# Zero rows under the last key block, later reciprocals and a fourth step masked on VectorE in a top-k attention and expert kernel

## The chip, the cores and the metric

The kernel runs on one core of a Trainium2 chip. What is timed is the device time of one execution, in microseconds (us). TensorE is called PE here, VectorE DVE, ScalarE ACT, GpSimd POOL and SyncE SP, as the profile does. PEld is the weight load of a matmul, SPq the queue of transfers that SP issues.

## What is computed

Attention over 2 batches and 8 heads, 576 tokens, 64 numbers a head, in which each token keeps its 32 best scores; then a sum over four experts with given shares; then a gated layer. All is float32.

```
scores = scale * np.matmul(q, k.transpose(0, 1, 3, 2))
kth = np.partition(scores, -32, axis=-1)[..., -32:-31]
scores = np.where(scores >= kth, scores, -1e9)
attn = np.exp(scores - scores.max(-1, keepdims=True))
attn = attn / (attn.sum(-1, keepdims=True) + 1e-09)
x = (attn @ v) as 1152 x 512
for e in range(4): y += p[:, e:e+1] * (relu(x @ w1[e]) @ w2[e])
out = ((y @ w_a) * (y @ w_b)) @ w_out
```

## The kernel before, in words

The 1152 tokens are nine tiles of 128: four of each batch, and a mixed one (MIX) with the last 64 tokens of both batches. The tiles stand in four groups of 1, 2, 3 and 3. Attention runs in 36 **steps**, numbered from 0: for each group, for each of the four pairs of heads, for each tile of the group. So steps 0 to 3 are group 0, 4 to 11 group 1, 12 to 23 group 2, 24 to 35 group 3.

One step does this for both heads of its pair. `scores` (L553) multiplies queries and keys on PE and ACT copies the result out of PSUM (L582). `masked` (L587) finds the 32 best of each of the 128 rows on DVE, by four MAX8 (L603, eight best at a time) and three MATCH_REPLACE8 (L609, which strikes them out) for each head. POOL makes the two row constants (L649); ACT and POOL push every score below the 32nd far down (L656, L659), ACT takes the exponent and its sum (L666), POOL adds 1e-9 (L675), DVE takes the reciprocal (L676), ACT scales (L679). The result is called e here. `weigh` (L686) turns e on PE (five matmuls against an identity for each head, L365), ACT copies it out (L706, L710), and PE multiplies it with the values (L726). The keys of a head are four blocks of 128 and a rest of 64: the rest's matmuls use 64 rows of the array, the other blocks 128. All these matmuls of `weigh` fill 64 of the 128 columns, two heads side by side. After the last tile of a pair the sum goes to `xf` (group 0) or, split into a high and a low part, to `xs` (the other groups, L744 on ACT, L746 on DVE).

Step 3 is marked URGENT. Its POOL work is done on DVE instead and its ACT work goes ahead of everything else, since its end lets PE begin on the expert layer of group 0.

The expert layer follows group by group: `plain` (L888) for group 0 in full float32, with weights in the regions `raw` and `ys`; `experts` (L817) for the others, with weights split into two parts by ACT (L767) and by POOL or DVE (L768), and results taken out by ACT (L837) and DVE (L841, L859). A group's first expert matmuls need all four pairs' `xs`. `replace` turns a group's result back, and `gated` is the last layer.

The order is not written out by hand. Every piece is recorded as an `Op` with an engine, a modelled duration (`hold`), a lag until others see it, a key and its waits; `Plan.order` (L91) plays the pieces through with these durations, picks on each engine the ready one of lowest key, and emits the instructions of each engine in the order in which they came up. Attention has keys near its step's number, copies out of PSUM negative ones, expert work 500 and more. On the chip each engine then runs its list strictly in that order and waits on semaphores. DVE's list thus mixes top-k work with the copies of the expert layer, and PE's mixes attention with expert matmuls. SP's list holds all transfers, in order too.

Of the kernel before, what the change touches and what calls it, by code (L numbers as in the profile page):

```python
# [8 lines left out]
F32 = mybir.dt.float32  # L9
# [57 lines left out]
class Op:  # L67
    __slots__ = ("engine", "hold", "lag", "key", "emit", "waits", "after", "tiles", "n", "start", "left", "at", "nbytes", "port")
# [7 lines left out]
class Plan:  # L76
# [3 lines left out]
    def add(self, engine, hold, emit, key, after=(), tiles=(), lag=100, nbytes=0, port=False):  # L80
# [4 lines left out]
        op.after, op.n, op.start, op.nbytes, op.port = [], len(self.ops), None, nbytes, port  # L85
# [5 lines left out]
    def order(self):  # L91
        for op in self.ops:
            op.left, op.at = len(op.waits), 0.0
            for w in op.waits:
                w.after.append(op)
# [17 lines left out]
        queue, now, done = [], 0.0, []  # L113
# [124 lines left out]
PAIRED, URGENT = (), 3  # L238


def body(tc, q, k, v, probs, w1, w2, wa, wb, wo, out):
# [50 lines left out]
    vrem = [const(f"vrem{b}", [REM, H, D]) for b in range(B)]  # L292
# [14 lines left out]
    raw = Region("raw", 3 * 1024, F32)  # L307
    wraws = raw.slots("wraw", 3, 1024)
    low = Region("low", 12800, F32)
# [34 lines left out]
    def load(dst, src, key, after=(), tiles=(), nbytes=1 << 18):  # L344

        return plan.add("SP", 0, lambda: nc.sync.dma_start(out=dst(), in_=src()), key, after, tiles, nbytes=nbytes)
# [37 lines left out]
    def consts():  # L384
        make_identity(nc, ident)
        nc.vector.tensor_copy(identr, ident)
        nc.gpsimd.memset(qm.bitcast(F32), 0.0)
        nc.gpsimd.memset(facs[:, :, 0], -scale)
        nc.gpsimd.memset(facs[:, :, 1], STEEP)

    ready = gpsimd(1900, consts, -1e6, (), ())

    loads = []
    for i, t in enumerate(TILES):
        for rows_, view in token_rows(t, probs):
            loads.append(load(lambda i=i, rows_=rows_: pr[rows_, i], lambda view=view: view, 2.0, nbytes=4096))
# [7 lines left out]
    shared = vector(900, shares, 3.5, loads, ())  # L404
# [13 lines left out]
    def keys(b, h2, key, eng):  # L418
# [7 lines left out]
        if first_:  # L426
            sp = [split(lambda j=j: sv()[:, j, :, 0], lambda j=j: sv()[:, j, :, 1], lambda j=j: rv()[:, j], 256, key, [ld], [rt, st_], eng) for j in range(2)]
# [18 lines left out]
        for j in range(2):  # L446
            at = atts.tile(key + 0.02)
# [7 lines left out]
            o = tensor(5 * TURN_R, turn, key + 0.02, sp[j] + krem_done[b][h + j] + [ready], [at, st_])  # L455
# [7 lines left out]
        if any(c for c, g in enumerate(GROUPS) if (b, h2) not in kept and c >= 0):  # L463
            kept[b, h2] = load(
                lambda: kscr[b, h2], lambda: kt.ap.rearrange("p (j n) -> p j n", j=2).bitcast(F32), key + 1, got, [kt], 576 << 10
# [11 lines left out]
    def start_pair(c, h2, n):  # L477
# [32 lines left out]
        for j in range(2):  # L510
            src = lambda j=j: rqv()[:, j].unsqueeze(2).to_broadcast([128, m, 2, D])
            sp[j] += split(lambda j=j: sqv()[:, j, 0:m, 0], lambda j=j: sqv()[:, j, 0:m, 1], src, m * 128, key + 0.03, lds, [rq, sq], eng)
            if m < T:
                if not qrem_done:
                    for b in range(B):
                        qrem_done.append(load(lambda b=b: qrem[b * REM:(b + 1) * REM], lambda b=b: last_rows(q, b), key - 2, (), (), 131072))
# [26 lines left out]
        for b in batches(tiles):  # L543
# [3 lines left out]
                lambda vt=vt: vt.ap.rearrange("p (h m d) -> p h m d", h=2, m=M4), lambda b=b: main_rows(v, b, h), n - 2.5, (), [vt]  # L547
            )]
            if b not in vrem_done:
                vrem_done[b] = load(lambda b=b: vrem[b], lambda b=b: last_rows(v, b), n - 2.4, (), (), 131072)  # L550
        return pair

    def scores(pair, j, i, n):  # L553
# [24 lines left out]
        o = tensor(4 * len(bs) * mm_r(HALF), emit, n - AHEAD, after, [at] + used)  # L578
# [503 lines left out]
```

## Time and profile before

| | us |
|---|---|
| median of 3 runs (867.55 to 869.35) | 867.97 |
| the profiled execution, its time | 866.53 |
| its span in the profile | 864.7 |
| PE busy in the span | 826.5 |
| DVE busy | 715.8 |
| ACT busy | 544.6 |
| POOL busy | 265.2 |

A busy share is a mean over stages with different limits. The profile cuts the span into 40 slices; in the first three PE is busy for 5, 5 and 7 tenths, and then for 9 tenths or more (90% and above) in nearly all others. The view by line names the program's line, the engine, the operation, the tiles written and read, the count, busy time, and the idle time ahead of it. The timeline lists instructions by their start, with like neighbours merged; the bracket gives the idle time of that engine before the row and what ended it.

### The profile page before, as it was taken

Reading aid. Unit: us, or ns where it says so; the run is one execution under the profiler, and the core shown is the slowest. Engines: PE = TensorE matmul, PEld = TensorE weight load, DVE = VectorE, ACT = ScalarE, POOL = GpSimd, SP = SyncE. Lnnn points to the kernel's source line nnn. Section 1 sums busy time; section 2 is a strip of 40 time slices with the busy share of each in tenths; the row PEclk is TensorE's granted clock in tenths of the full one; section 3 lists DMA queues with packets and bytes.
Section 4 is the critical chain, followed back from the end, with each engine's and each line's share of the span. In section 5 each row is a group of like instructions: output and inputs, shape, how many; then the busy total and the mean of one; then the engine's idle time right before and its main releaser. Section 6 shows DMA issues by size and latency. Waiting matters only on the chain. (4 is left out here: it accounts for less than half of the span.)

```text
span 864.7 us, 14129 instructions
## 1 busy us (share of the span) xinstructions
PE 826.5 (96%) x5168; PEld 728.0 (84%) x5168; DVE 715.8 (83%) x1381; ACT 544.6 (63%) x1042; POOL 265.2 (31%) x245
## 2 busy tenths in 40 slices
PE   5579999999999999999999999999999999999997
PEld 4466777788888888889888888889999989999996
DVE  6899999999999999999978999555434888999723
ACT  5888987899989998877765655333324535344310
POOL 2634442887897965853320000000000000000000
PEclk9999999999999999999999999999999999999999
DMA  7727977844564444342234556434101313323003
GB/s 197 244 90 257 297 239 235 268 149 145 168 185 150 152 148 153 98 123 97 75 122 156 179 177 195 122 122 128 44 1 49 98 49 98 91 81 98 25 1 109
DMA packets 83509, 117.06 MB, mean 135 GB/s; under 512 B 10608, under 2 KB 54640, under 8 KB 83440
## 3 DMA queue, kind: packets, MB, share of 16 engines
q1 hardware_dynamic: 83440, 116.17, 42.9%
q8 instruction: 40, 0.66, 0.3%
q14 instruction: 29, 0.24, 0.1%
HBM read 109.07 MB, written 7.08 MB: 134 GB/s over the span
## 5 line engine op out<-in xcount | busy, mean ns | idle before, releaser
L603 DVE MAX8 low<-low 128x8 f32<-128x576 f32 x288 | 203.7, 747 | 3.4 <-ACT low L582 3.3
L362 PE MATMUL ps<-xs,mid 128*128 128x384 f32 (+1 forms) x1152 | 205.1, 322 | 1.3 <-POOL mid L768 1.0
L362 PE MATMUL ps<-mid 128*128 128x512 f32 x768 | 198.6, 396 | 2.1 <-DVE mid L841 2.0
L362 PEld LDWEIGHTS ps<-xs,mid 128*128 128x128 f32 x1152 | 184.4, 189 | 11.5 <-issue 2.5
L362 PEld LDWEIGHTS ps<-mid 128*128 128x128 f32 x768 | 139.2, 188 | 28.5 <-DVE mid L841 6.0
L609 DVE MATCH_REPLACE8 low<-low 128x576 f32<-128x576 f32 x216 | 159.3, 743 | 0.0
L362 PE MATMUL ps<-xs,big 128*128 128x384 f32 x864 | 152.8, 335 | 0.0
L362 PEld LDWEIGHTS ps<-xs,big 128*128 128x128 f32 x864 | 149.9, 188 | 1.6 <-DVE low L1033 0.3
L767 ACT ACTIVATE mid<-raw 128x1024 fp32r<-128x1024 f32 x96 | 101.5, 1059 | 66.3 <-issue 39.9
L768 POOL TENSOR_TENSOR mid<-raw,mid 128x1024 fp32r<-128x1024 f32 x48 | 115.2, 2408 | 11.9 <-ACT mid L767 8.9
L659 POOL TENSOR_TENSOR low<-low 128x576 f32<-128x576 f32 x70 | 98.9, 1428 | 32.8 <-ACT low L656 31.0
L362 PE MATMUL ps<-big,mid 128*128 128x512 f32 x324 | 75.1, 390 | 0.0
L768 DVE TENSOR_TENSOR mid<-raw,mid 128x1024 fp32r<-128x1024 f32 x48 | 58.5, 1220 | 18.9 <-ACT mid L767 18.7
L362 PEld LDWEIGHTS ps<-big,mid 128*128 128x128 f32 x324 | 60.7, 188 | 12.3
L837 ACT ACTIVATE mid<-ps 128x384 fp32r<-128x384 f32 (+1 forms) x96 | 42.7, 450 | 33.0 <-PE ps L362 28.3
L859 DVE SCALAR_TENSOR_TENSOR ys<-ps,pr,ys 128x512 f32<-128x512 f32 x56 | 41.5, 747 | 24.3 <-PE ps L362 23.7
L841 DVE SCALAR_TENSOR_TENSOR mid<-ps,mid 128x384 fp32r<-128x384 f32 (+1 forms) x96 | 48.0, 506 | 15.1 <-ACT mid L837 14.6
L656 ACT ACTIVATE low<-low 128x576 f32<-128x576 f32 x72 | 53.4, 772 | 7.6 <-POOL low L649 7.4
L1012 ACT ACTIVATE low<-ps 128x384 f32<-128x384 f32 x36 | 17.6, 489 | 64.1 <-PE ps L362 64.0
L365 PE MATMUL ps<-ident,low 128*128 128x128 f32 (+1 forms) x360 | 50.6, 282 | 7.3 <-ACT low L679 7.1
L679 ACT ACTIVATE low<-low 128x576 f32<-128x576 f32 x72 | 52.9, 776 | 6.1 <-DVE low L676 6.1
L666 ACT ACTIVATE low<-low 128x576 f32<-128x576 f32 x72 | 55.7, 774 | 0.7 <-POOL low L659 0.7
(76 smaller groups left out, 1040.0 us busy)
## 6 DMA issues: line engine op xcount, KB each, us to landing
raw<-in_moe_w_dram SPq DMA_DIRECT2D x120, 512.0 KB, 3.7
big<-kscr SPq DMA_DIRECT2D x20, 576.0 KB, 4.8
low<-in_v_dram SPq DMA_DIRECT2D x24, 256.0 KB, 4.1
low<-in_moe_w_a_dram SPq DMA_DIRECT2D x12, 512.0 KB, 3.8
low<-in_moe_w_b_dram SPq DMA_DIRECT2D x12, 512.0 KB, 3.8
low<-in_moe_w_out_dram SPq DMA_DIRECT2D x12, 512.0 KB, 3.6
kscr<-big SPq DMA_DIRECT2D x8, 576.0 KB, 4.4
ys<-in_moe_w_dram SPq DMA_DIRECT2D x8, 512.0 KB, 4.6
```

Of the source, the lines that this page charges most:

```text
L362: nc.tensor.matmul(out, l, r, **kw)
L365: nc.tensor.transpose(out, a, i)
L603: 62 + 1.04 * width, lambda at=at, cs=cs: nc.vector.max(m8v()[:, x, cs], at()), key + 0.02 * r, [done],
L609: lambda at=at, cs=cs: nc.vector.match_replace(out=src[1](), in_to_replace=m8v()[:, x, cs], in_values=at(), imm_value=LOW),
L656: S, lambda x=x, s=s: nc.scalar.activation(e[x].ap, s.ap, AF.Relu, bias=endv()[:, x, 1:2], scale=-STEEP),
L659: sub = lambda eng, x=x, s=s: eng.tensor_tensor(e[x].ap, s.ap, e[x].ap, op=ALU.subtract)
L666: lambda x=x: nc.scalar.activation(e[x].ap, e[x].ap, AF.Exp, bias=endv()[:, x, 0:1], scale=scale, accum_out=sums.ap[:, x:x + 1]),
L679: S, lambda x=x: nc.scalar.activation(e[x].ap, e[x].ap, AF.Copy, scale=sums.ap[:, x:x + 1]),
L767: hi = scalar(1024, lambda: nc.scalar.activation(u.ap[:, 0:1024], r.ap, AF.Copy), 500 + s, [ld], [u, r], sbuf=True)
L768: sub = lambda eng: eng.tensor_tensor(u.ap[:, 1024:2048], r.ap, u.ap[:, 0:1024], op=ALU.subtract)
L837: n, lambda h=h, p=p: nc.scalar.activation(h.ap[:, 0:n], p.ap[:, 0:n], AF.Relu), -1000, [o], [h, p]
L841: lambda h=h, p=p: nc.vector.scalar_tensor_tensor(h.ap[:, n:2 * n], p.ap[:, 0:n], 0.0, h.ap[:, 0:n], op0=ALU.max, op1=ALU.subtract),
```

## The change

- **Zero rows.** The tiles of the rest of the values (`vrem`) get 128 rows, and rows 64 to 127 of it and of the last block of the turned e (`pt`) are set to zero once, on POOL, near the start (five memsets). The matmuls of `weigh` on the rest use 128 rows of the array like the others. `weigh` waits for the zeros.
- **Later reciprocals.** The planner is told that the sum of a step is seen 1200 ns later (2400 ns for steps 0 and 1), so DVE's reciprocal stands later in its list. Its key is lower for steps 0 to 2.
- **Step 3 masked on DVE.** ACT takes the exponent of all scores as soon as the first eight maxima are known. After the last MAX8 DVE does, for each head, one SCALAR_TENSOR_TENSOR (score at least the 32nd, times the exponent, with the row sum), adds 1e-9, takes the reciprocal and scales with a TENSOR_SCALAR. The turn of its e gets a key ahead of most other PE work, and the ACT and POOL work of steps 0 to 2 gets lower keys.
- **Loads by time.** A transfer can be held back to a planned time (`since`): shares at 30 us, values from 9 us on, the weights of group 0 from 20 us on, the stored keys at 13 us, the queries' rest at 60 us.
- **Two engines evict first.** In step 0 DVE takes over two of the four copies out of PSUM that ACT did, the keys of the second head and the queries of the first, and the operands are split head by head.
- **Fourth weight place.** `raw` holds 4 tiles, not 3; room comes from the second identity and from `low`. Every fifth weight tile of group 0 goes to `ys`, not every fourth.
- **Planned durations.** The turn of a key pair is planned at 640 ns (440 before), of e at 516 (476), scores with 30 more, `weigh` at 1245 (1150).
- **Early units.** `experts` takes a weight unit out of a table `ahead` if there is one. Nothing is ever put into that table.

The diff, cut to its core:

```diff
-        queue, now, done = [], 0.0, []
+        queue, now, done = [(op.since, -1, None) for op in self.ops if op.since], 0.0, []
...
-    ident = const("ident", [128, 128])
     identr = const("identr", [128, 128], F32R)
+    ident = identr.bitcast(F32)
...
-    vrem = [const(f"vrem{b}", [REM, H, D]) for b in range(B)]
+    vrem = [const(f"vrem{b}", [128, H, D]) for b in range(B)]
...
-    raw = Region("raw", 3 * 1024, F32)
-    wraws = raw.slots("wraw", 3, 1024)
+    raw = Region("raw", 4 * 1024, F32)
+    wraws = raw.slots("wraw", 4, 1024)
...
+    def zeros():
+        for b in range(B):
+            nc.gpsimd.memset(vrem[b][REM:128], 0.0)
+        for p in pts.aps:
+            nc.gpsimd.memset(p[REM:128, MAIN:MAIN + 128], 0.0)
+    zeroed = gpsimd(1500, zeros, 0.2, [ready], ())
...
+            if first_ and j == 1:
+                got.append(vector(
+                    dve(S),
+                    lambda j=j, at=at: nc.vector.tensor_copy(kt.ap[:, j * S:(j + 1) * S], at.ap.rearrange("p a n -> p (a n)")[:, 0:S]),
+                    -902 + j, [o], [at, kt],
+                ))
+                continue
...
+        ks = n + 0.1 if n > URGENT else n - 0.7
...
+        sm.lag += 2 * SLACK if n < URGENT - 1 else SLACK
+        rc = vector(70, lambda: nc.vector.reciprocal(sums.ap, sums.ap), -500 if n > URGENT else -3500, [sm], [sums])
...
+    def hurried(sd, n, m8v, m8, ends, endv, sums, firsts, last):
...
+            ex = scalar(
+                S, lambda x=x, s=s, e=e: nc.scalar.activation(e.ap, s.ap, AF.Exp, bias=endv()[:, x, 0:1], scale=scale),
+                n + 0.1, [en], [s, e, ends], sbuf=True, ptr=True,
+            )
+            sv = lambda x=x: sums.ap[:, x:x + 1]
+
+            def mask(x=x, s=s, e=e, sv=sv):
+                nc.vector.scalar_tensor_tensor(
+                    e.ap, s.ap, m8v()[:, x, TOPK - 1:TOPK], e.ap, op0=ALU.is_ge, op1=ALU.mult, accum_out=sv()
+                )
+                nc.vector.tensor_scalar(sv(), sv(), 1e-9, None, op0=ALU.add)
+                nc.vector.reciprocal(sv(), sv())
+                nc.vector.tensor_scalar(e.ap, e.ap, sv(), None, op0=ALU.mult)
+            out_.append((e, vector(1450, mask, -3000, [ex, last[x]], [s, e, m8, sums], port=True)))
...
-            at, p = atts.tile(n + 0.5), pts.tile(n)
+            kt = n + (-0.06 if n == URGENT else 0.5)
+            at, p = atts.tile(kt), pts.tile(n)
...
-                        l, rows = (vt[:, j, m], 128) if m < M4 else (vrem[b][:, pair.h + j], REM)
+                        l = vt[:, j, m] if m < M4 else vrem[b][:, pair.h + j]
                         mm(
-                            ov()[j * D:(j + 1) * D, i, r0:r1], l, pt[j].ap[0:rows, m * 128 + r0:m * 128 + r1],
+                            ov()[j * D:(j + 1) * D, i, r0:r1], l, pt[j].ap[:, m * 128 + r0:m * 128 + r1],
...
-            1150, emit, n + 0.6, ptd + sum((pair.vd[b] for b in bs), []) + [vrem_done[b] for b in bs], [pair.o] + pt + [pair.v[b] for b in bs]
+            1245, emit, n + 0.6, [zeroed] + ptd + sum((pair.vd[b] for b in bs), []) + [vrem_done[b] for b in bs], [pair.o] + pt + [pair.v[b] for b in bs]
```

**Where instructions move, first place: DVE at the end of step 3's top-k.** In these rows `low` holds scores, maxima, e and sums, and `prs` and `pr` the experts' shares. MAX and MATCH_REPLACE are the top-k; the reciprocal of two columns ahead of the shares is step 2's. Before, from that reciprocal on:

```order
L676 RECIPROCAL low<-low 128x2
L609 MATCH_REPLACE low<-low 128x576 x2
L603 MAX low<-low 128x8 x2
L399 TENSOR_REDUCE prs<-pr 128x9
L400 TENSOR_SCALAR prs<-prs 128x9
L401 RECIPROCAL prs<-prs 128x9
L402 TENSOR_TENSOR pr<-pr,prs 128x36
L603 MAX low<-low 128x8
L659 TENSOR_TENSOR low<-low 128x576 x2
L603 MAX low<-low 128x8
```

Now, from step 3's last two MAX on:

```order
L633 MAX low<-low 128x8 x2
L414 TENSOR_REDUCE prs<-pr 128x9
L415 TENSOR_SCALAR prs<-prs 128x9
L416 RECIPROCAL prs<-prs 128x9
L417 TENSOR_TENSOR pr<-pr,prs 128x36
L680 RECIPROCAL low<-low 128x2
L704 SCALAR_TENSOR_TENSOR low<-low 128x576
L707 TENSOR_SCALAR low<-low 128x1
L708 RECIPROCAL low<-low 128x1
L709 TENSOR_SCALAR low<-low 128x576
L704 SCALAR_TENSOR_TENSOR low<-low 128x576
L707 TENSOR_SCALAR low<-low 128x1
```

Step 2's reciprocal moved behind step 3's last MAX and behind the shares; the two subtractions of step 3 are gone, and the two masks stand ahead of step 4's first MAX.

**Second place: PE at the hand-over from group 1 to group 2.** `mid` holds weights and hidden values of the expert layer, `xs` the attention's result; 128x256 are matmuls of group 1, 128x384 of group 2. The matmuls of `low` against the identity are the turn of e, here of step 23 (the last of its group). Before:

```order
L362 MATMUL ps<-xs,mid 128x256 x39
L362 MATMUL ps<-mid 128x512 x3
L362 MATMUL ps<-xs,mid 128x256 x3
L362 MATMUL ps<-mid 128x512 x12
L365 MATMUL ps<-ident,low 128x128 x4
L365 MATMUL ps<-ident,low 64x128
L365 MATMUL ps<-ident,low 128x128 x4
L365 MATMUL ps<-ident,low 64x128
L362 MATMUL ps<-mid 128x512 x6
```

Now:

```order
L368 MATMUL ps<-xs,mid 128x256 x36
L368 MATMUL ps<-mid 128x512 x3
L368 MATMUL ps<-xs,mid 128x256 x3
L368 MATMUL ps<-mid 128x512 x18
L368 MATMUL ps<-xs,mid 128x384 x3
L368 MATMUL ps<-mid 128x512 x3
L368 MATMUL ps<-xs,mid 128x384 x12
L371 MATMUL ps<-identr,ys 128x128 x2
L368 MATMUL ps<-xs,mid 128x384 x3
L371 MATMUL ps<-identr,low 128x128 x4
L371 MATMUL ps<-identr,low 64x128
```

All matmuls of group 1, 18 of group 2 and two turns of group 1's result now stand ahead of step 23's turn; before, nine of group 1 stood behind it.

Three more counts from the two lists. PE: ahead of the first matmul on the last quarter of `xf` stand 48 score matmuls (128x288), 56 before; ahead of step 35's turn stand 387 matmuls of 512 columns from `mid`, 393 before, and all else alike. DVE: ahead of step 23's reciprocal stand 204 MAX, 153 MATCH_REPLACE and 48 copies out of the expert layer, before 202, 151 and 45.

## Rows read from the trace of the kernel before

**Rows 1.** The page: busy time; 40 slices; a group: count | busy us, mean ns | idle before.

```profile
PE 826.5 (96%) x5168; PEld 728.0 (84%) x5168; DVE 715.8 (83%) x1381; ACT 544.6 (63%) x1042; POOL 265.2 (31%) x245
...
PE   5579999999999999999999999999999999999997
...
L362 PE MATMUL ps<-mid 128*128 128x512 f32 x768 | 198.6, 396 | 2.1 <-DVE mid L841 2.0
```

**Rows 2.** Busy us (x instructions) of each engine in two stretches, then PEclk, DMA share, GB/s.

```profile
0.00:66.34 66.34, 43.42 (x282) 35.37 (x282) 55.19 (x122) 50.88 (x112) 26.24 (x42) 0.97 0.59 176
66.34:299.09 232.75, 227.19 (x1696) 189.66 (x1697) 225.66 (x488) 204.28 (x406) 157.67 (x131) 1.00 0.65 205
```

**Rows 3.** Timeline of DVE: start us, us, line, operation, [idle before <-what ended it].

```profile
9.45 0.76 DVE L603 MAX8 low<-low 128x8 f32<-128x576 f32 x1 [3.11 <-ACT low L582]
...
29.98 0.17 DVE L676 RECIPROCAL low<-low 128x2 f32<-128x2 f32 x1 [2.90 <-POOL low L675]
...
42.31 0.17 DVE L676 RECIPROCAL low<-low 128x2 f32<-128x2 f32 x1 [0.86 <-POOL low L675]
...
50.37 0.17 DVE L676 RECIPROCAL low<-low 128x2 f32<-128x2 f32 x1 [0.36 <-POOL low L675]
...
53.22 0.17 DVE L399 TENSOR_REDUCE prs<-pr 128x9 f32<-128x36 f32 x1
...
54.00 0.76 DVE L603 MAX8 low<-low 128x8 f32<-128x576 f32 x1
54.67 1.41 DVE L659 TENSOR_TENSOR low<-low 128x576 f32<-128x576 f32 x2
```

**Rows 4.** By line on DVE: count | busy us, mean ns | idle before, what ended it.

```profile
L676 DVE RECIPROCAL low<-low 128x2 f32<-128x2 f32 x35 | 5.5, 156 | 5.2 <-POOL low L675 5.1
L971 DVE TENSOR_SCALAR low<-low 128x512 f32<-128x512 f32 x36 | 15.2, 422 | 10.3 <-ACT low L970 10.3
```

**Rows 5.** Timeline of PE, steps 2 and 3 of attention.

```profile
51.40 1.43 PE L365 MATMUL ps<-ident,low 128*128 128x128 f32 x10 [1.45 <-ACT low L679]
...
62.90 1.67 PE L362 MATMUL ps<-big 128*128 128x288 f32 x8
64.50 1.09 PE L362 MATMUL ps<-low 128*64 128x128 f32 x16
...
66.34 1.16 PE L362 MATMUL ps<-xf,raw 128*128 128x128 f32 x8 [0.38 <-ACT xf L738]
```

**Rows 6.** Timeline of PE, one step's multiplication with the values, instruction by instruction.

```profile
202.31 0.50 PE L362 MATMUL ps<-low 128*64 128x128 f32 x6
...
202.52 0.28 PE L362 MATMUL ps<-low 128*64 128x128 f32 x2
202.73 0.33 PE L362 MATMUL ps<-low,vrem 64*64 64x128 f32 x2
...
203.10 0.80 PE L362 MATMUL ps<-big 128*128 128x288 f32 x4
```

**Rows 7.** Timeline of PE where a step of the mixed tile multiplies with the values.

```profile
333.64 0.69 PE L362 MATMUL ps<-low 128*64 128x64 f32 x16
334.25 0.33 PE L362 MATMUL ps<-low,vrem 64*64 64x64 f32 x4
334.52 0.69 PE L362 MATMUL ps<-low 128*64 128x64 f32 x16
```

**Rows 8.** Timeline of PE at the turns of steps 23 and 35.

```profile
299.09 1.25 PE L365 MATMUL ps<-ident,low 128*128 128x128 f32 x10
...
452.33 0.77 PE L365 MATMUL ps<-ident,low 128*128 128x128 f32 x5 [0.72 <-ACT low L679]
```

**Rows 9.** Waits of DVE from 54 to 452 us: who for whom, us in total, times, longest.

```profile
DVE mid L841 <- ACT mid L837: 5.4, 8, 1.5
DVE ys L859 <- PE ps L362: 3.0, 9, 0.5
DVE xs L746 <- ACT xs L744: 2.4, 3, 1.6
```

More of the change, by code (lines that the diff above doesn't have):

```diff
@@ L67 @@
 class Op:
-    __slots__ = ("engine", "hold", "lag", "key", "emit", "waits", "after", "tiles", "n", "start", "left", "at", "nbytes", "port")
+    __slots__ = ("engine", "hold", "lag", "key", "emit", "waits", "after", "tiles", "n", "start", "left", "at", "nbytes", "port", "since")
 SEEN, SEEN_PE = 45, 130
@@ L84, in add @@
         op.tiles = list({id(t): t for t in tiles}.values())
[L85 removed]
+        op.after, op.n, op.start, op.nbytes, op.port, op.since = [], len(self.ops), None, nbytes, port, 0.0
         for t in op.tiles:
@@ L92, in order @@
         for op in self.ops:
-            op.left, op.at = len(op.waits), 0.0
+            op.left, op.at = len(op.waits), op.since
             for w in op.waits:
@@ L341, in body, with load @@
     os_ = Slots("o", [ps[:, 7]])
-    def load(dst, src, key, after=(), tiles=(), nbytes=1 << 18):
-        return plan.add("SP", 0, lambda: nc.sync.dma_start(out=dst(), in_=src()), key, after, tiles, nbytes=nbytes)
+    def load(dst, src, key, after=(), tiles=(), nbytes=1 << 18, since=0.0):
+        op = plan.add("SP", 0, lambda: nc.sync.dma_start(out=dst(), in_=src()), key, after, tiles, nbytes=nbytes)
+        op.since = since
+        return op
     def scalar(n, emit, key, after, tiles, sbuf=False, ptr=False, extra=0):
@@ L426, in keys @@
         if first_:
-            sp = [split(lambda j=j: sv()[:, j, :, 0], lambda j=j: sv()[:, j, :, 1], lambda j=j: rv()[:, j], 256, key, [ld], [rt, st_], eng) for j in range(2)]
+            sp = [split(lambda j=j: sv()[:, j, :, 0], lambda j=j: sv()[:, j, :, 1], lambda j=j: rv()[:, j], 256, key + 0.032 * j, [ld], [rt, st_], eng) for j in range(2)]
         else:
@@ L446, in keys @@
         for j in range(2):
-            at = atts.tile(key + 0.02)
+            at = atts.tile(key + 0.02 + 0.01 * j)
             def turn(j=j, at=at):
@@ new lines, in masked @@
+            last.append(top(x, [lambda s=s: s.ap, lambda x=x: e[x].ap], 0, TOPK // 8, S, key, sd[x][1]))
+        if urgent:
+            return hurried(sd, n, m8v, m8, ends, endv, sums, firsts, last)
+        ks = n + 0.1 if n > URGENT else n - 0.7
+        out_, ex = [], []
+        en = gpsimd(
+            150, lambda: nc.gpsimd.tensor_tensor(endv(), m8v()[:, :, ::TOPK - 1], facs, op=ALU.mult), -500, last + [ready], [m8, ends]
+        )
+        for x in range(2):
+            s = sd[x][0]
+            a = scalar(
+                S, lambda x=x, s=s: nc.scalar.activation(e[x].ap, s.ap, AF.Relu, bias=endv()[:, x, 1:2], scale=-STEEP),
+                ks, [en], [s, e[x], ends], sbuf=True, ptr=True,
+            )
+            b = gpsimd(
+                pool_(S), lambda x=x, s=s: nc.gpsimd.tensor_tensor(e[x].ap, s.ap, e[x].ap, op=ALU.subtract), ks, [a], [s, e[x]]
+            )
+            ex.append(scalar(
+                S,
+                lambda x=x: nc.scalar.activation(
+                    e[x].ap, e[x].ap, AF.Exp, bias=endv()[:, x, 0:1], scale=scale, accum_out=sums.ap[:, x:x + 1]
+                ),
+                ks, [b], [e[x], ends, sums], sbuf=True, ptr=True, extra=92,
+            ))
```

142 lines of the change are left out of this document (56 added, 86 removed).

## The prediction

> **What bounds the kernel now.** I began with the page. PE is busy for 96% of the span, and its 40 slices show where the rest is: 5, 5 and 7 tenths in the first three, 9 and more after that [rows 1]. So the end is set by PE's work plus the time that it loses near the start. Then the view by stretches, cut at 66.34 us, where PE starts on the last quarter of `xf` [rows 5]; I call this point T0. Up to T0 PE is busy for 43.42 of 66.34 us, so it idles for 22.9. In the next 232.75 us it idles for 5.6 [rows 2]. Before T0 it has only attention to do, and after T0 the expert layer of group 0 fills every gap. The granted clock is 0.97 and 1.00 of full speed in the two stretches, the upper level of 2.4 GHz nearly throughout, so the clock is no term here.
>
> What holds T0 back is on DVE's timeline [rows 3]. Its first MAX8 starts at 9.45, and the top-k of steps 0 to 3 runs almost without a break until 53.22. Breaks stand ahead of the reciprocals of steps 0, 1 and 2: 2.90, 0.86 and 0.36, all waits for POOL. DVE's list is in order, so a reciprocal whose sum is not there holds up the top-k behind it. From 53.22 it takes 13.1 us more to T0.
>
> After T0 there are two full streams. DVE is busy for 225.7 of 232.75 us, PE for 227.2 [rows 2]. They meet where PE's list has the turn of some step's e: steps 23 and 35, the last of groups 2 and 3, at 299.09 and 452.33, the second after a wait of 0.72 [rows 8]. A gain on PE counts only if DVE's top-k comes earlier as well.
>
> **The sum is made against the profiled execution**, 866.53 us with a span of 864.7; the median of the three runs, 867.97, lies 1.44 above it, and I give times on the median's scale. A difference under 0.2%, 1.7 us, could not be told from none.
>
> **The start.** Two copies leave ACT's list and run on DVE beside it. The trace does not show the pair side by side. The gain lies between nothing and the whole wait ahead of the first MAX8, 3.11 [rows 3]. I take 0.6, near the lower end, since transfers, splits and matmuls of that chain stay. The five memsets on POOL, and the held-back loads, lie in a stretch where PE is half idle and POOL is busy for 26.2 of 66.3 us [rows 2]. I cost them at nothing; without that cover the first split on POOL would be late, and with it step 1's scores.
>
> **The reciprocals.** Behind later work they find their sums ready: 2.90 + 0.86 + 0.36 = 4.1 us up to T0 [rows 3], and of the 5.2 on all 35 [rows 4] another 1.1 later. With the 0.6, step 3's last MAX8 ends at 53.2 - 4.7 = 48.5.
>
> **Step 3 on DVE.** SCALAR_TENSOR_TENSOR over 576 is not in the trace; the nearest row is the pair of subtractions over 576, 1.41 for two [rows 3], so 0.7. TENSOR_SCALAR takes 0.42 over 512 [rows 4], so 0.47 over 576. The four small operations of the shares fill 53.22 to 54.00 [rows 3], so 0.2 each. One head costs 0.7 + 0.2 + 0.2 + 0.47 = 1.6, both 3.1. Gone are the two subtractions (1.4) and four small operations that partly overlapped (0.5). DVE pays 1.2 net; 0.5 if the small ones cost half, 2 if the accumulation adds 0.4 to each.
>
> **T0.** The masks end at 48.5 + 0.8 (shares) + 0.1 + 3.1 = 52.5. But step 2's reciprocal now stands behind the shares, at 49.3, and PE's list has step 2 ahead of step 3. From reciprocal to turn it took 51.40 - 50.37 = 1.03 [rows 3, 5], so step 2's turn starts at 50.4, only 1.0 earlier than before. Behind it stand on PE: that turn (1.3 to the next instruction), eight score matmuls (1.6), step 2's values (1.4), step 3's turn (1.1 without waits), the turn of two key heads (ten matmuls like the turn of e, 1.2, and 0.6 until the places of step 3's turn are copied out), step 3's values (1.4) and the copy to `xf` (0.4) [rows 5]: 9.0. So T0 comes at 59.4, 6.9 earlier. If step 2 were not in front, the masks alone would allow 55.5; if only the DVE gain of 4.7 came through, 61.6. I take 59.4, as it follows PE's list piece by piece. Eight score matmuls (56 before, 48 now ahead of T0) have moved behind it and cost about 1.2 there, where the clock is full. Net **5.7 us**.
>
> **Zero rows.** One step's values [rows 6]: pairs of matmuls start 0.105 apart (202.31 to 202.52). From the last pair on 128 rows to the first on 64 it is 0.21, and the two pairs on 64 rows take 0.37 up to the next instruction. With 128 rows throughout, the first 0.21 becomes 0.105 and the 0.37 becomes 0.105 plus the way out. If leaving costs the same 0.21 as entering, the step saves 0.105 + 0.055 = 0.16; the bounds are 0.105 (the way out keeps all) and 0.265 (it costs nothing). The mixed tile [rows 7]: 16 matmuls in 0.61, a pair in 0.076; the two pairs on 64 rows take 0.27 against 0.15, so 0.12 for each batch and 0.25 a step. After T0 come 28 plain and 4 mixed steps: 28 x 0.16 + 4 x 0.25 = **5.5 us**.
>
> The Trainium skill's page "TensorE: Matmul & The Clock Gate", section "Why this matters for your kernels", says that a matmul on 32 rows takes as long as one on 128 and that small ones gain only by running side by side. By that rule the rows themselves are worth nothing and the sum would be 5.7; the trace's 0.21 against 0.105 speaks for the change of shape as the cost.
>
> **Can DVE follow?** Up to step 35 it gains 0.6 + 4.1 + 1.1 - 1.2 = 4.6 for certain. It also loses 10.8 us in waits from 54 to 452 in three groups [rows 9], all for results that trace back to PE. The planner put one step's values at 1.15 us, and they take about 1.4 (ten pairs at 0.105 and the two changes); now it plans 1.245 where 1.23 is due. So PE will no longer come later than DVE's list assumes, and I expect three quarters of these waits, 8 us, to go. Step 23's turn: PE's list has nine matmuls of 512 columns (0.26, from 198.6 / 768 [rows 1]), 18 of 384 (in proportion 0.19) and two small ones more ahead of it, 6.0 us. PE comes there at 299.1 - 5.7 - 3.0 (19 steps of zero rows) + 6.0 = 296.4. DVE has 4 top-k instructions (0.67 each: a MAX8 from 54.00 to 54.67 [rows 3]) and three copies more ahead of its reciprocal, about 4.5, which eats the 4.6; with half of the 8 us its e is there at 295. Step 35's turn: DVE allows 452.3 - 12.6 = 439.7, and PE comes at about 452.3 - 5.7 - 5.2 - 1.6 (six matmuls fewer) = 439.8. The two streams stay level, and PE's own sum holds: 5.7 + 5.5 = **11.2 us**, hence 867.97 - 11.2 = **856.8**. The fourth weight place is worth nothing in itself, since no wait of PE in the trace ends on a transfer. The table of early units is never filled and changes nothing.
>
> **Rivals.**
> - *DVE keeps its waits* (20%). Then step 35's turn comes 4.6 earlier, PE still has 1.6 us more behind it, less 0.2 of zero rows: 3.2 us, **864.8**. For it: DVE is as full as PE [rows 2]. Against it: the waits are for PE [rows 9].
> - *The rows are worth nothing* (8%): the 0.105 is the price of other weights and stays. 11.2 - 5.5 = 5.7, **862.3**. For it speaks the skill's page named above; against it, equal tiles in the same step change weights at 0.105 [rows 6].
> - *PE loses its own gaps too* (10%): of the 5.6 us up to 299.09 [rows 2] all go as the plan fits. 11.2 + 5.6 = 16.8, **851.2**.
> - *PE waits at every turn* (7%), the way to slower. The reciprocal stands later in DVE's list, and PE's list turns e where the plan expects it. If the plan is a little early, PE stops at each of the 32 steps after T0. At 0.5 us, less than the 0.72 that step 35 shows [rows 8], that costs 16 and leaves +4.8: **872.8**. It decides from 11.2 / 32 = 0.35 us a step. Against it: before, few turns waited, and the lag is put into the plan.
> - *Parts cancel* (3%): about 868.
>
> My forecast has the remaining 52%, with its own range of 851 to 861 from the bounds of T0 (55.5 to 61.6) and of the zero rows (0.105 to 0.265). The range of 8 in 10 takes in the third rival and the first: **850.5 to 865**. A tenth of the first rival falls within 1.7 us. Faster 0.88, same 0.05, slower 0.07.
>
> **What would show it.** T0 near 59.4; no wait of DVE at its first three reciprocals; step 3's last MAX8 ending near 48.5; two masks of about 1.6; the values of a step in 1.23 and no 64-row matmul; the DVE waits of rows 9 down to about 3. I am wrong if T0 is after 62, if PE idles for more than 7 us between T0 and step 35's turn, or if the first matmul on the rest starts 0.2 after the last full pair.

## The result and the profile after

| | before | changed |
|---|---|---|
| time, median (runs) | 867.96 us (867.55 to 869.35, 4) | 856.72 us (854.94 to 859.79, 4) |
| ratio to before, 95% interval | | 0.9871 [0.9835, 0.9908] |
| profiled execution; its span | 866.53; 864.7 us | 854.94; 853.2 us |
| T0, PE's start on the last quarter of `xf` | 66.34 us | 60.18 us |

The kernel is faster by 11.2 us in the medians and by 11.6 in the profiled executions; the forecast was 856.8. First the page of the changed kernel: PE's total and its 40 slices.

```profile
PE 818.9 (96%) x5168; PEld 726.6 (85%) x5168; DVE 717.9 (84%) x1387; ACT 539.5 (63%) x1034; POOL 265.4 (31%) x250
...
PE   6689999999999999999999999999999999999997
```

PE is busy for 7.6 us less than in [rows 1], and the slices that are not full are still the first three and the last. The view by stretches, cut at T0 and at the turns of steps 23 and 35 (columns as in [rows 2]):

```profile
0.00:60.18 60.18, 40.52 (x274) 33.63 (x275) 55.03 (x124) 46.05 (x100) 25.95 (x44) 0.86 0.62 184
60.18:295.28 235.10, 230.63 (x1734) 195.65 (x1734) 232.00 (x500) 207.18 (x414) 165.23 (x140) 1.00 0.67 213
295.28:440.50 145.22, 143.24 (x1040) 127.83 (x1039) 138.97 (x276) 118.85 (x242) 74.23 (x68) 1.00 0.36 114
440.50:853.20 412.70, 404.46 (x2124) 369.48 (x2122) 291.93 (x490) 167.38 (x281) 0.00 (x0) 1.00 0.31 95
```

PE idles for 19.7 us before T0 instead of 22.9, and the granted clock there is 0.86 instead of 0.97 [rows 2]. Between T0 and step 35's turn DVE idles for 3.1 + 6.25 = 9.4 us. Before it was 7.1 [rows 2] and 9.4 in the stretch between the two turns, 16.5 in all:

```profile
299.09:452.33 153.24, 151.60 (x1075) 134.40 (x1074) 143.80 (x285) 122.08 (x246) 81.28 (x73) 1.00 0.36 116
```

DVE's timeline up to T0 answers to [rows 3]:

```profile
8.90 0.76 DVE L633 MAX8 low<-low 128x8 f32<-128x576 f32 x1 [1.50 <-ACT low L613]
...
28.34 0.14 DVE L680 RECIPROCAL low<-low 128x2 f32<-128x2 f32 x1
...
38.77 0.17 DVE L680 RECIPROCAL low<-low 128x2 f32<-128x2 f32 x1
...
47.83 0.18 DVE L414 TENSOR_REDUCE prs<-pr 128x9 f32<-128x36 f32 x1
...
49.05 0.15 DVE L680 RECIPROCAL low<-low 128x2 f32<-128x2 f32 x1
49.13 0.79 DVE L704 SCALAR_TENSOR_TENSOR low<-low 128x576 f32<-128x576 f32 x1
...
50.79 0.81 DVE L704 SCALAR_TENSOR_TENSOR low<-low 128x576 f32<-128x576 f32 x1
...
52.47 1.41 DVE L633 MAX8 low<-low 128x8 f32<-128x576 f32 x2
```

None of the three reciprocals has a wait ahead of it, and step 3's top-k ends at 47.83. The masks run from 49.13 to 50.79 and from there to 52.47, 1.66 and 1.68 us. PE's timeline from step 2's turn to T0, and its turns of steps 23 and 35, answer to [rows 5, 8]:

```profile
50.07 2.40 PE L371 MATMUL ps<-identr,low 128*128 128x128 f32 x10 [1.98 <-ACT low L683]
...
53.73 1.09 PE L368 MATMUL ps<-low 128*64 128x128 f32 x16
54.66 0.39 PE L368 MATMUL ps<-low,vrem 128*64 128x128 f32 x4
54.98 1.31 PE L371 MATMUL ps<-identr,low 128*128 128x128 f32 x10
...
60.18 1.12 PE L368 MATMUL ps<-xf,raw 128*128 128x128 f32 x8
...
295.28 1.25 PE L371 MATMUL ps<-identr,low 128*128 128x128 f32 x10
...
440.50 1.25 PE L371 MATMUL ps<-identr,low 128*128 128x128 f32 x10
```

A step's values take 54.98 - 53.73 = 1.25 us and hold no matmul on 64 rows; step 35's turn no longer waits. DVE's waits up to step 35's turn answer to [rows 9], and are alike in two executions of the changed kernel: 10.8 us in the three kinds became 3.9.

```profile
DVE mid L874 <- ACT mid L870: 2.7, 4, 1.9
...
DVE ys L892 <- PE ps L368: 0.6, 3, 0.2
DVE xs L778 <- ACT xs L776: 0.6, 1, 0.6
```

The next wait of the second kind, 1.95 us at 442.50, lies behind that turn; the expectation of the old durations below counts it in and says 5.9.

### The profile page after: what moved, and what is told of

Same layout as the page of the kernel before. It is cut to its first block, busy times and chain, and to the rows that moved or that the text cites. A ratio compares the mean times of both kernels' runs of the same rounds, so it can differ in the third digit from the quotient of the medians.

```text
span 853.2 us, 14162 instructions
## 1 busy us (share of the span) xinstructions
PE 818.9 (96%) x5168; PEld 726.6 (85%) x5168; DVE 717.9 (84%) x1387; ACT 539.5 (63%) x1034; POOL 265.4 (31%) x250
## 4 chain that ended last, share of the span: by engine, by line
PE 73%; DVE 15%; ACT 5%; issue 3%; POOL 2%; DMA 1%; DVEq 0%; POOLq 0%; ACTq 0%
PE ps L368 68%; PE ps L371 5%; DVE low L633 4%; DVE low L641 4%; DVE mid L800 2%; DVE mid L874 1%; ACT mid L799 1%; ACT low L664 1%; POOL low L668 1%; DVE ys L892 1%; DMA raw<-in_moe_w_dram 1%; POOL big L428 1%; ACT low L613 1%; ACT low L683 1%; ACT low L672 0%
## 5 line engine op out<-in xcount | busy, mean ns | idle before, releaser
L368 PEld LDWEIGHTS ps<-xs,mid 128*128 128x128 f32 x1152 | 183.9, 188 | 14.7 <-DVE mid L874 4.4
L683 ACT ACTIVATE low<-low 128x576 f32<-128x576 f32 x70 | 51.4, 776 | 11.4 <-DVE low L680 11.3
L870 ACT ACTIVATE mid<-ps 128x384 fp32r<-128x384 f32 (+1 forms) x96 | 43.1, 452 | 22.0 <-PE ps L368 15.1
L664 ACT ACTIVATE low<-low 128x576 f32<-128x576 f32 x70 | 52.8, 778 | 4.3 <-POOL low L658 4.2
L672 ACT ACTIVATE low<-low 128x576 f32<-128x576 f32 x70 | 54.5, 779 | 0.7 <-POOL low L668 0.7
L613 ACT ACTIVATE low<-ps 128x576 f32<-128x576 f32 x72 | 46.5, 650 | 12.5 <-PE ps L368 6.6
```

The lines of the kernel that those rows point to most:

```text
L368: nc.tensor.matmul(out, l, r, **kw)
L613: S, lambda: nc.scalar.activation(s.ap.rearrange("p (c n) -> p c n", c=2), at.ap[:, :, 0:HALF], AF.Copy),
L664: S, lambda x=x, s=s: nc.scalar.activation(e[x].ap, s.ap, AF.Relu, bias=endv()[:, x, 1:2], scale=-STEEP),
L672: lambda x=x: nc.scalar.activation(e[x].ap, e[x].ap, AF.Exp, bias=endv()[:, x, 0:1], scale=scale, accum_out=sums.ap[:, x:x + 1]),
L683: S, lambda x=x: nc.scalar.activation(e[x].ap, e[x].ap, AF.Copy, scale=sums.ap[:, x:x + 1]),
```

## The experiments

All were timed in 5 rounds beside the kernel before, whose median was 867.1 to 868.6 us in these comparisons. "Changed" is the changed kernel.

**The changed kernel itself**, to have it beside the others on one chip.

> The changed kernel once more, as the mark for the others on the same chip. The four runs so far lie in two pairs, near 855 and near 859. Expected: a median of 855 to 859, T0 (start of the matmuls on the last quarter of xf) near 60.2, the turn of step 23 near 295 and of step 35 near 441. If the spread of 4 us comes from the chip and not from the kernel, the runs on this chip agree within 1 us.

Measured: 856.2 us, ratio 0.9863 [0.9845, 0.9881]. The four runs lie within 1.2 us. T0 is 61.07 in this profile, and the span 855.1. The differences below are from this 856.2. By the ratios they come out up to 0.7 us otherwise: 6.0 and 4.8 for the zero rows undone and alone, 1.6 for the old durations, 0.5 for the reciprocals, 4.7 for step 3's scale, 15.1 for the loads, 6.3 for more work on DVE, 3.9 for values first.

**Zero rows, undone and alone.**

```diff
-l = vt[:, j, m] if m < M4 else vrem[b][:, pair.h + j]
+l, rows = (vt[:, j, m], 128) if m < M4 else (vrem[b][0:REM, pair.h + j], REM)
...
-l, pt[j].ap[:, m * 128 + r0:m * 128 + r1],
+l, pt[j].ap[0:rows, m * 128 + r0:m * 128 + r1],
```

> The changed kernel with the matmuls on the rest of the keys on 64 rows again; plan, order, zeros and everything else kept. Theory (the change of the array's shape costs PE time, and PE sets the end after T0): a step's values take 1.40 instead of 1.25, and the end comes 28 x 0.15 + 4 x 0.25 = 5.2 us later than the unchanged copy, about 862. Rival 1 (the step is hidden, because DVE's top-k sets the pace up to step 35): under 2 us later. Rival 2 (rows are worth nothing): no difference, and the first matmul on the rest starts 0.10 after the last full pair as now.

Alone, in the kernel before (with `zeros()` and `vrem` of 128 rows):

```diff
-l, rows = (vt[:, j, m], 128) if m < M4 else (vrem[b][:, pair.h + j], REM)
+l = vt[:, j, m] if m < M4 else vrem[b][:, pair.h + j]
...
-ov()[j * D:(j + 1) * D, i, r0:r1], l, pt[j].ap[0:rows, m * 128 + r0:m * 128 + r1],
+ov()[j * D:(j + 1) * D, i, r0:r1], l, pt[j].ap[:, m * 128 + r0:m * 128 + r1],
```

> The kernel before with the zero rows alone: five memsets and 128 rows in the last matmuls; order and planned durations as before. Theory (PE sets the end, and before DVE waited for PE as well): 35 steps x 0.15 and the mixed ones, all after T0: 5.2 us faster, 862.8, and DVE's waits for PE shrink below the 10.8 of three groups. Rival (DVE's top-k sets the pace up to step 35): the gain shows only from step 35 on, under 1.5 us.

Measured: undone 862.7 us, 0.9932 [0.9914, 0.995], 6.5 above the changed kernel; alone 863.14 us, 0.9945 [0.9927, 0.9962], 5.4 below before. Both agree with the term of 5.5. Alone, the zero rows take little of DVE's waits: the three kinds of [rows 9] still make 9.5. PE's timeline of the undone kernel, step 2's values:

```profile
53.12 1.09 PE L368 MATMUL ps<-low 128*64 128x128 f32 x16
54.15 0.43 PE L368 MATMUL ps<-low,vrem 64*64 64x128 f32 x4
54.52 1.31 PE L371 MATMUL ps<-identr,low 128*128 128x128 f32 x10
```

Here the step takes 1.40 us, with 128 rows 1.25. Of the 0.15, 0.10 lies ahead of the first matmul on 64 rows (1.03 against 0.93) and 0.05 from there to the next instruction (0.37 against 0.32). So it is the change of shape that costs, and at most 0.05 of it can be the rows. The Trainium skill's page "TensorEngine Tiling (Array Packing)", section "Tiling Modes", says that changing the tiling mode drains the engine; the trace agrees in that the change costs time, 0.15 us for the way in and out.

**The old planned durations** in the changed kernel; likewise for the two kinds of turn (`5 * TURN_R`, `4 * TURN_F + 40`).

```diff
-o = tensor(4 * len(bs) * mm_r(HALF) + 30, emit, n - AHEAD, after, [at] + used)
+o = tensor(4 * len(bs) * mm_r(HALF), emit, n - AHEAD, after, [at] + used)
...
-    1245, emit, n + 0.6, [zeroed] + ptd + sum((pair.vd[b] for b in bs), []) + [vrem_done[b] for b in bs], [pair.o] + pt + [pair.v[b] for b in bs]
+    1150, emit, n + 0.6, [zeroed] + ptd + sum((pair.vd[b] for b in bs), []) + [vrem_done[b] for b in bs], [pair.o] + pt + [pair.v[b] for b in bs]
```

> The changed kernel with the planned durations of before (440, 476, scores without the 30, 1150), all else kept; the order comes out anew. Theory (the plan now fits PE, so that DVE's list no longer assumes PE too early): DVE's waits for PE between T0 and step 35 grow from 5.9 to 9 or more, and the end comes 3 to 8 us later, 860 to 865. Rival (the durations only shuffle): within 2 us of the unchanged copy.

Measured: 858.05 us, 0.9882 [0.9864, 0.99], 1.9 above. The three kinds of DVE's waits come to 7.4 us up to step 35's turn (3.7, 2.0 and 1.7), against 3.9, so about half of what went comes back. The time hardly follows: what I had named as the cause that would free DVE of its waits is worth at most 1.9 us.

**The reciprocals where they stood before.**

```diff
-SLACK = 1200
+SLACK = 0
...
-rc = vector(70, lambda: nc.vector.reciprocal(sums.ap, sums.ap), -500 if n > URGENT else -3500, [sm], [sums])
+rc = vector(70, lambda: nc.vector.reciprocal(sums.ap, sums.ap), -500, [sm], [sums])
```

> The changed kernel with one part undone: the sums' reciprocals stand in DVE's order where they stood before (no slack after the sums, the old key). Theory (the reciprocal stalls held T0 back): the stalls of rows 3 return, together 3 to 4 us before T0; but step 2's reciprocal now stands ahead of the shares, so that not all of it reaches T0: T0 at 62 to 64 instead of 60.2 to 61.1, another 1 us is lost later, and the time is 2.5 to 4.5 above the changed kernel's 856.2 to 856.7. Rival (the stalls were covered, T0 came from step 3's masks alone): stalls return, T0 and the time move by less than 1 us.

Measured: 856.2 us, 0.9869 [0.985, 0.9888], no different from the changed kernel. DVE's timeline, the first three reciprocals:

```profile
27.47 0.17 DVE L680 RECIPROCAL low<-low 128x2 f32<-128x2 f32 x1 [0.94 <-POOL low L677]
...
37.98 0.17 DVE L680 RECIPROCAL low<-low 128x2 f32<-128x2 f32 x1 [0.71 <-POOL low L677]
...
49.31 0.17 DVE L680 RECIPROCAL low<-low 128x2 f32<-128x2 f32 x1
```

With the other parts in place the stalls are 1.65 us, not 4.1 [rows 3], and step 2's reciprocal, now ahead of step 3's last two MAX8, comes 0.26 us later than in the changed kernel. T0 is 60.32. The rival holds. The planner also wrote other lists, and the masks of step 3 run from 50.71 to 54.51, 2 us later than in the changed kernel; T0 did not move with them. So T0 hangs on step 2's turn, not on the masks, which have some 2 us of room.

**Step 3's scale as before** (Relu, subtraction on DVE, Exp and Copy for each head, in place of what `hurried` does; its ACT work goes ahead of everything else again, and the early place of its turn on PE stays).

```diff
...
-out_.append((e, vector(1450, mask, -3000, [ex, last[x]], [s, e, m8, sums], port=True)))
+b = vector(dve(S), lambda e=e, s=s: nc.vector.tensor_tensor(e.ap, s.ap, e.ap, op=ALU.subtract), -3000, [a], [s, e], port=True)
...
+out_.append((e, scalar(
+    S, lambda x=x, e=e, sv=sv: nc.scalar.activation(e.ap, e.ap, AF.Copy, scale=sv()),
+    -3000, [rc], [e, sums], sbuf=True, ptr=True,
+)))
```

> The changed kernel with step 3's scale done as before: per head Relu on ACT, subtraction on DVE, Exp and Copy on ACT, in place of the mask on DVE; the early place of its turn in PE's order stays. Theory (my sum: step 3's last MAX8 at 48 plus the 13.1 us that the old chain took to T0): T0 at 61 to 62.5, and the time 0.5 to 2.5 above the changed kernel. Rival (the mask brought most of the T0 gain): T0 at 63.5 or later, time 3 or more above. Second rival (step 2 alone sets T0): T0 as in the changed kernel, time within 0.7.

Measured: 860.27 us, 0.9917 [0.9901, 0.9933], 4.1 above, T0 at 66.08: the first rival, 1.6 us over the most that my sum allowed. ACT's timeline shows where it begins:

```profile
49.37 0.76 ACT L683 ACTIVATE low<-low 128x576 f32<-128x576 f32 x1
50.04 0.76 ACT L698 ACTIVATE low<-low 128x576 f32<-128x576 f32 x1
50.70 0.76 ACT L703 ACTIVATE low<-low 128x576 f32<-128x576 f32 x1
...
52.10 0.77 ACT L703 ACTIVATE low<-low 128x576 f32<-128x576 f32 x1
...
52.86 0.76 ACT L683 ACTIVATE low<-low 128x576 f32<-128x576 f32 x1
53.52 1.43 ACT L710 ACTIVATE low<-low 128x576 f32<-128x576 f32 x2
```

The two Copies of step 2 (L683) stand 3.49 us apart, with step 3's Relu and Exps between them; in the changed kernel both run in one piece from 49.24. PE's turn of step 2 is cut in two for that, as its timeline shows:

```profile
50.19 1.33 PE L371 MATMUL ps<-identr,low 128*128 128x128 f32 x5 [1.63 <-ACT low L683]
53.67 1.33 PE L371 MATMUL ps<-identr,low 128*128 128x128 f32 x5 [2.16 <-ACT low L683]
```

The second half of that turn starts at 53.67; in the changed kernel PE is past the whole turn at 52.12. The rest of the 5.9 us by which T0 is later comes behind it, where PE also runs at half clock. From 50 to 60.18 us, the changed kernel first:

```profile
50.00:60.18 10.18, 10.11 (x94) 9.31 (x95) 10.01 (x26) 7.19 (x18) 1.25 (x1) 0.85 0.36 98
50.00:60.18 10.18, 7.10 (x35) 5.86 (x37) 10.18 (x26) 7.64 (x17) 0.20 (x1) 0.51 0.06 14
```

So 4.1 us is what the old form costs with all that follows from it. How much of that is ACT's list and how much the clock is not separated; the five runs do not follow their mean clock (859.83 at 0.977, 860.27 at 0.993, 861.72 at 0.989).

**Loads as soon as a place is free**, in `load`:

```diff
-op.since = since
+op.since = 0.0
```

> The changed kernel with the plan's start times of loads set to zero: values, gates, kept keys, shares and weights are issued as soon as a place is free, as before. Theory (I costed the start times at nothing): first MAX8 within 0.3 of 8.9, time within 1.7 of the changed kernel. Rival (the transfers of the start collide without them): first MAX8 later by over 0.5, T0 later by over 2, time 2 or more above.

Measured: 870.93 us, 1.0037 [1.0023, 1.0052], 14.7 above the changed kernel and slower than before. I had costed this part at nothing. The first MAX8 is where it was (8.90), but POOL's first split starts at 12.56 instead of 10.49, since the first values and two loads of the shares go ahead of the second keys on SP, and the planner writes other lists for all engines. In DVE's list step 2's reciprocal now stands behind the first mask of step 3, which waits for its Exp:

```profile
52.14 0.82 DVE L704 SCALAR_TENSOR_TENSOR low<-low 128x576 f32<-128x576 f32 x1 [2.40 <-ACT low L698]
...
53.82 0.16 DVE L680 RECIPROCAL low<-low 128x2 f32<-128x2 f32 x1
```

T0 is 65.26. The rest is lost behind it. Against the changed kernel the span is 15.9 us longer: T0 5.1, PE idle behind T0 4.8 more (19.5 against 14.7), PE busy behind T0 6.0 more (784.4 against 778.3). Of these 6.0, about 4.5 are clock, by an estimate from three stretches: behind gaps of PE (1.6 us ending at 169.31, 0.8 and 1.95 up to 255.04, 2.2 up to 503.92) the granted clock falls in part to its lower level, 1.2 GHz. Busy time by stretches:

```profile
172.00:180.00 8.00, 8.00 (x56) 7.41 (x56) 7.11 (x17) 7.25 (x15) 6.46 (x5) 0.85 0.53 176
...
255.00:259.50 4.50, 4.46 (x15) 3.56 (x16) 3.84 (x8) 3.73 (x5) 4.34 (x4) 0.65 0.48 143
...
503.90:512.00 8.10, 8.08 (x34) 7.32 (x35) 6.46 (x13) 2.71 (x6) 0.00 (x0) 0.79 0.41 129
```

0.15 x 8.0 + 0.35 x 4.5 + 0.21 x 8.1 = 4.5 us. The largest gap behind T0 in the changed kernel, 1.65 up to 491.40, is followed by a clock of 1.00.

**More work on DVE.**

```diff
+if n > URGENT and x == 0 and r == 0:
+    nc.vector.max(m8v()[:, x, cs], at()[:, 0:128])
 nc.vector.max(m8v()[:, x, cs], at())
```

> The changed kernel with one MAX8 over 128 columns more in each of steps 4 to 35 on DVE, ahead of the step's first MAX8 and without effect on the result; planned durations and order as in the changed kernel. Each should take about 0.2 us, 6.4 us over 32 steps. DVE is idle for 9.4 us from T0 to step 35's turn. Theory (PE alone sets the end and DVE has that much room): time less than 2 above the changed kernel. Rival (the two streams are level, as the turn of step 35 suggested): 4 to 6.5 above, with PE waiting for turns of e.

Measured: 861.88 us, 0.9936 [0.9918, 0.9953], 5.7 above `again`. By line on DVE the added MAX8 take 0.28 us each, not 0.2:

```profile
L631 DVE MAX8 low<-low 128x8 f32<-128x128 f32 x32 | 8.9, 279 | 0.4 <-ACT low L613 0.4
```

DVE is busy for 8.1 us more in all (726.0 against 717.9), and its idle time from T0 to step 35's turn fell from 9.4 to 7.2 us only; PE's idle time there grew from 6.4 to 10.6. The rival holds: the streams are level, and the idle time that DVE has left there is not room.

**What of loads_any_time is the order on SP?** Two kernels in which SP's list alone is rearranged by hand, behind the planner.

```diff
...
+vs = [op for op in sp if op.part == "v"][:4] + [op for op in sp if op.part == "vrem"][:1]
+at = done.index(sp[4])
+for op in done[:at] + vs + [op for op in done[at:] if op not in vs]:
     op.emit()
```

> The changed kernel with one thing moved by hand, in SP's list alone: the four loads of values and one of the last rows of values that belong to the start are issued ahead of the second load of keys, as in the kernel before; every other engine's list is that of the changed kernel. It tells apart what of the 14.7 us of loads_any_time is the order on SP and what the other lists that the plan makes without start times. Theory (order of the transfers): the second pair of key heads is split 2 us later, POOL's first split at 12.5 instead of 10.5, T0 at 63 or later, time 4 or more above the changed kernel. Rival (the lists of the engines): the split is 2 us later as well, but DVE's top-k is behind by some time of its own, so T0 moves by 1.5 at most and the time by less than 2.5.

```diff
...
+vs = sp[4:10]
+at = done.index(sp[12]) + 1
+for op in [op for op in done[:at] if op not in vs] + vs + done[at:]:
     op.emit()
```

> The kernel before with one thing moved by hand, in SP's list alone: the second and third loads of keys and the second of queries are issued ahead of the first loads of values, last rows of values and shares; every other list is that of the kernel before. Theory (order of the transfers): POOL's first split at about 10.4 instead of 12.4, the reciprocal's stall of 2.90 shrinks by 1 to 2, T0 earlier by 1 to 3, time 1 to 4 less than the kernel before. Rival (lists, not transfers): the split comes earlier, DVE's first reciprocal still waits for POOL about as long, T0 within 0.7 and the time within 1 of the kernel before.

Measured: values first in the changed kernel 859.87 us (856.49 to 860.73), 0.9908 [0.9887, 0.9928], 3 to 4 above; the profiled execution, one of the shortest, has T0 at 61.18 and POOL's split at 11.46. Neither bound is met clearly: the order on SP is worth a part, far from all of the 14.7. Values late in the kernel before: 868.4 us, 1.0014 [1.0002, 1.0026], no gain, T0 even at 69.37. The split comes at 11.09, but DVE's first reciprocal waits 4.58 us.

**The loads of the shares out of the way too**, in the kernel before (`fourth` is the fourth load of keys, `late` the first of kept keys, `prs_` the loads of the shares).

```diff
...
+if op in vs or op in prs_:
+    continue
+out_.append(op)
+if op is fourth:
+    out_ += vs
+if op is late:
+    out_ += prs_
```

> The kernel before with SP's list alone rearranged by hand, in the way of the changed kernel: the second and third loads of keys and the second and third of queries come ahead of the first values, and the ten small loads of the shares, which in values_late_alone still took SP from 9.6 to 17.5 ahead of a load of queries, come behind the first kept keys at 28 us. Every other list is that of the kernel before. Theory (what is issued on SP ahead of keys and queries makes step 0's sum late, and start times for loads are worth much in themselves): DVE's first reciprocal waits less than 1.5 instead of 2.90, T0 at 62 to 65 instead of 66.3, time 2 to 5 less than the kernel before. Rival (the transfers help only with lists that use them): the queries come earlier, DVE's stalls become shorter, but T0 moves by 1.5 at most and the time by less than 1.5.

Measured: 869.48 us, 1.0023 [1.001, 1.0036]: worse, and neither theory, as the stall grew. ACT's timeline and DVE's name the chain:

```profile
28.07 0.51 ACT L409 ACTIVATE big<-low 128x128 fp32r<-128x128 f32 x2 [3.01 <-DMA low<-in_q_dram]
28.48 0.76 ACT L666 ACTIVATE low<-low 128x576 f32<-128x576 f32 x1
```

```profile
31.50 0.17 DVE L676 RECIPROCAL low<-low 128x2 f32<-128x2 f32 x1 [4.36 <-POOL low L675]
```

Step 0's Exp (L666) stands in ACT's list behind a split of queries of a later step, and these queries, issued on SP at 22.48 behind values and the first weights (before: at 20.54), land late. A late load thus reaches DVE through ACT's Exp and POOL's sum. Whether it helps to take loads from in front when that one comes early as well was not tried.

**One exchange in the lists of loads_any_time.**

```diff
...
+dv = [op for op in done if op.engine == "DVE"]
+m = next(i for i, op in enumerate(dv) if op.key == -3000)
+r = next(op for op in dv[m:] if op.key == -3500)
+done.remove(r)
+done.insert(done.index(dv[m]), r)
```

> The kernel of loads_any_time with one thing moved by hand, in DVE's list alone: step 2's reciprocal stands ahead of the first mask of step 3 instead of behind it. In loads_any_time the mask waited 2.4 us for its Exp on ACT, and the reciprocal, whose sum was ready, stood behind it, with step 2's turn on PE (54.9 instead of 50.1). Theory (that list is what held T0 back): step 2's turn at 51 to 52, T0 at 62 to 63.5 instead of 65.3, time 2 to 3.5 below loads_any_time (870.9). Rival (step 3's late Exp holds T0): T0 and time within 1 of loads_any_time.

Measured: 870.9 us (867.29 to 875.43), 1.0038 [1.002, 1.0057], the same time as without the exchange. T0 came to 63.02, step 2's turn to 53.83: a part of what the theory asked, and the end did not follow. The expectation had the sum ready, but the reciprocal, at 51.82, now waits 2.32 us for POOL. In loads_any_time ACT reads the second sum of step 2's Exp at 50.94, in the changed kernel at 46.52: so step 2 is late already on ACT, whatever DVE's list holds. The gaps behind T0 are all there again (255.04 became 256.19, 503.92 became 505.14).

## The parts put together

T0 and the span behind it, from one profiled execution of each kernel:

| kernel | T0, us | span - T0, us |
|---|---|---|
| before | 66.34 | 798.4 |
| values_late_alone, loads_late_alone | 69.37, 69.27 | 799.2, 798.5 |
| zeros_alone | 65.93 | 794.5 |
| changed, again | 60.18, 61.07 | 793.0, 794.0 |
| old_durations, recip_early | 61.54, 60.32 | 795.1, 792.5 |
| values_first, step3_old | 61.18, 66.08 | 793.5, 791.9 |
| rows64 | 59.87 | 797.9 |
| dve_extra | 61.20 | 799.9 |
| loads_any_time, recip_swapped | 65.26, 63.02 | 803.8, 807.3 |

Behind T0 the kernels without zero rows need 798 to 799 us, those with them 792 to 795, wherever T0 lies between 59.9 and 69.4. So the sum of the prediction had the right form: T0, and what PE has to do behind it. The last two lines are the exceptions: more work on DVE, and lists that leave PE gaps.

## Why the prediction was right, and where its reasons were not

- **T0** 59.4 forecast, 60.18 and 61.07 measured; net of the eight score matmuls 5.7 forecast, 4.1 to 5.0 measured (their 1.2 is an estimate, and no run shows it alone). Along the way: first MAX8 0.55 sooner (0.6), step 3's top-k at 47.83 (48.5), shares 1.22 (0.8), masks 1.66 and 1.68 (1.6), step 2's turn at 50.07 (50.4), a step's values 1.25 (1.23). That T0 follows step 2's turn through PE's list was read rightly, but from that turn to T0 it took 10.1 us, not 9.0. "Before T0 it has only attention to do" left out the eight matmuls on the third quarter of `xf` between step 3's turn and the keys' (0.8), and "the clock is no term here" was wrong: from 50 to 52 us the granted clock is 0.50, and step 2's turn took 2.05 us, not 1.3. The 0.6 us of waiting for copies and some of the values' 1.4 were too much. With the clock at 1.00 in that stretch, in the run with early reciprocals, the same way took 60.32 - 51.13 = 9.2.
- **Zero rows** 5.5 forecast; 5.4 alone, 6.5 undone (4.8 and 6.0 by the ratios), 0.15 us a step on PE (0.16). The Trainium skill's page "TensorE: Matmul & The Clock Gate", section "Why this matters for your kernels", is not contradicted where it says that few rows take as long as many: what is saved is the change of shape, which that rule leaves out. The time that the prediction worked out by it, 862.3, did not come.
- **The attribution within T0 failed**, in three steps. "I cost them at nothing" was said of the held-back loads: without start times 14.7 us come back. "Behind later work they find their sums ready", for 4.1 us, was true of the stalls, but put back they cost nothing. "DVE pays 1.2 net" was said of the mask, whose old form I gave 0.5 to 2.5 us in its expectation: it costs 4.1, which begins in ACT's list. Each of start times and mask, taken away alone, moves T0 back to 65 or 66, nearly the whole gain. So the gain needs both, and what each costs when it is undone does not add up to it. My sum came out because it followed the last chain and not the edits.
- **DVE's waits.** "Three quarters of these waits, 8 us, to go" nearly held: 6.9 of 10.8 went, and DVE's idle time from T0 to step 35's turn fell from 16.5 to 9.4. The cause that I gave, planned durations, brings back 3.5 of these waits when undone and is worth at most 1.9 us of time. What else in the lists took the rest was not tried.
- **The turns** of steps 23 and 35 came at 295.28 and 440.50 (296.4, 439.8), and "the two streams stay level" was right: 0.15 us a step more on PE cost 6.5 us, 8.1 us more on DVE cost 5.7. The rivals "DVE keeps its waits" (864.8), "PE waits at every turn" (872.8) and "PE loses its own gaps too" (851.2) did not come; PE still idles for 4.5 us up to step 23's turn (5.6 before).
- **Luck.** That the forecast met the median within 0.1 us is luck: the four runs lie between 854.94 and 859.79, T0 came 0.8 to 1.7 us later than forecast, and the span behind T0 became 4.4 to 5.4 us shorter where the sum had 5.5 - 1.2 = 4.3.
- **Open:** which pieces of the lists that the planner writes without start times make the gaps behind T0. The five loads moved on SP explain about a quarter of the 14.7 us, step 2's reciprocal none of it. The ten loads of the shares, which in loads_any_time stand among the loads of keys and queries on SP, from 6.32 to 15.78 us, were not moved in the changed kernel. The two copies on DVE, the fourth weight place and the new keys of steps 0 to 3 were not undone by themselves either.

## What to carry to other kernels

Follow the last chain to the point from which the bounding engine is full, and add the change of its work behind that point; edits ahead of it that are all needed for one gain are not to be added up, and undoing one told more here than doing it alone. Where a planner writes the lists, an edit of its inputs, such as the time from which a load may start, is an edit of every list, and is worth a run of its own before it is costed at nothing. In an in-order list look at what an instruction stands behind: a late load of queries held up an Exp, a sum and a reciprocal on three other engines.

## What the runs showed of the hardware

- Gaps near 2 us in a nearly full PE can cost clock behind them. In loads_any_time gaps of 1.6 and 0.5, of 0.8 and 1.95, and of 2.2 us were followed by stretches at 0.85, 0.65 and 0.79 of full clock, an estimated 1.2, 1.6 and 1.7 us. In the changed kernel gaps of 0.5 and 1.65 up to 491.40 were followed by none. What decides is not shown.
- Ahead of T0 the low clock falls in other places from one execution to the next: in the changed kernel's profile at 30 to 34 and 50 to 52 us, in that of `again` at 44 to 52, each at 0.50. The mean up to 60 us is 0.86 and 0.91, yet T0 is 0.9 us later in `again`: there step 1's values took 1.76 us to their last four matmuls instead of 0.93, and ACT's copy to `xf` (48.49 against 46.62), step 2's Copies behind it (50.60 against 49.24) and step 2's turn (51.42 against 50.07) came later.
- Small loads are not cheap to issue: in loads_late_alone SP was at the ten loads of the shares, 1 or 2 KB each, for 8.28 us from 30.28, and at one load of weights of 512 KB for 0.43 at 24.74.
